# Opening of a gated-attention + GELU-FFN kernel on one Trainium2 core: hand-written engine orders, weight conversion as a stream, visits in two halves

## Chip, cores, metric

The kernel runs on one core of one Trainium2 chip. The metric is device time in microseconds (us). The kernel before took 604.11 us in the median of three runs (602.83 to 604.21). Engines are named as the profile names them: PE (TensorE), DVE (VectorE), ACT (ScalarE), POOL (GpSimd), SP (SyncE, which issues most of the transfers).

## What is computed

A linear attention with a decay per channel runs over 768 time steps for 4 batches and 8 heads of 48 channels; its output, seen as 3072 tokens of 384 channels, goes through a feed-forward network with an exact GELU. All in fp32.

```python
# attention, per batch and head, D = 48
state = alpha[t][:, None] * state + outer(k[t], v[t])
y[t]  = q[t] @ state
# FFN on x = y as 3072 x 384
h = x @ w_in                                   # 384 x 2048
g = 0.5 * h * (1 + erf(h / sqrt(2)))
out = g @ w_out                                # 2048 x 384
```

The weights reach the chip as float64 and are turned to fp32 pairs there.

## The kernel before, in words

**Groups, pairs, visits.** Time is cut into 12 groups of 256 steps (three groups per batch), and the heads into 4 pairs. For every group `g` and pair `p` there are three pieces of attention work. `st0` (L200), which `ahead` (L398) calls, is the preparation: two scans of alpha on DVE (`pp` L203, `rp` L209), a tiny maximum and reciprocal between them (L205, L208), and two products that scale k and q in place (L210, L212; from group 3 on the product for q is on POOL). A `visit` (L376) then works on three pairs at once, as a pipeline of depth three: for the newest pair `scores` and `turned` (PE, into the PSUM tile `s`), then `out_of_scores` (DVE mask product `ss` L240, ACT copy `kn` L247); for the pair before it `inside` (PE, into `ybank`) and `chain` (four small DVE adds `state` L318 to L322); for the pair before that `outside_part` (PE into `ybank`), `carry` (DVE L327) and `out_of_y` (ACT cast L365 and DVE residual L366, which leave x as a high and a low part). After the last pair of a group the tile `z` is scattered into the three x tiles of the group by six transfers on SP (`x<-z` L372), and only then can the FFN of that group begin.

**FFN steps.** The FFN is a list of 96 steps. A step (`ffn_step` L571) takes one group and one eighth of d_ff: `gemm1` is 18 matmuls into `hp` (L413), ACT takes two GELUs of it (`ghi` L422, and in place L423), DVE makes the low part `glo` (L424), and `gemm2` is 12 matmuls into two accumulators `acc` (L435). `gemm2` of a step is issued after `gemm1` of the next one. When a span of steps of one group ends, DVE moves the accumulators into `part` (L451, or L447 where it adds). The first three groups share out their eighths in spans of 4, 2 and 2, so that the weights are needed late. From step 12 (slot 25) on, visits are slotted between the gemms at the positions of `FIRST_VISITS` and then at every fourth slot, two slots to a step.

**Weight conversion.** A piece is 768 KB of float64 (one eighth of w_in or of w_out); there are 16. `split_weights` (L170) loads a piece into the staging tile `st`, ACT rescales its upper words (`u` L179), six DVE instructions assemble the fp32 value and its low part (L180, L181, L184, L185, L186, and L188 for the low part), and ACT casts the high part between the last two (L187). The results are the tiles `wih`, `wil`, `woh`, `wol`.

**What sets the order.** The program is written in one order; a planner with a timeline model then sets the order of instructions on each engine, up to step 12 on all of them. From there (`ON_PE`, L575) PE keeps the order as written. Each engine runs its own queue in order, so an instruction that waits holds all that stands behind it on that engine. SP carries the transfers and small marker instructions that keep blocks of matmuls on `ybank` apart (L264).

Of the kernel before, what the change touches and what calls it, by code (L numbers as in the profile page):

```python
# [24 lines left out]
RC = 1  # L25
STAGE = 2
WARM = 22
XB = 4
ON_PE = 12
AHEAD = 3  # L30
FIRST_VISITS = (25, 28, 31, 34, 37, 40)
EVERY = 4


@with_exitstack
def gla_then_gelu_ffn(ctx: ExitStack, tc: tile.TileContext, q, k, v, alpha, w_in, w_out, out):
# [52 lines left out]
    n_checks = NG - GPB + GPB * NPAIR // RC  # L89
# [52 lines left out]
    stage = stage_cm.__enter__()  # L142

# [26 lines left out]
    def split_weights(src, hi, lo, name):  # L170
        st = stage.tile([P, 2 * DM], I64, tag="st", name=f"st_{name}")
        nc.sync.dma_start(st.rearrange("p (two e) -> p two e", two=2), src)
        hi, lo = (x.rearrange("p two e -> p (two e)") for x in (hi, lo))
        top = st.bitcast(I32)[:, 1::2]
        mid = st.bitcast(U16)[:, 1::4]
        u = stage.tile([P, 2 * DM], F32, tag="u", bufs=1, name=f"u_{name}")
        w = stage.tile([P, 2 * DM], F32, tag="w", bufs=2, name=f"w_{name}")
        ui, wi = u.bitcast(I32), w.bitcast(I32)
        nc.scalar.activation(u, st.bitcast(F32)[:, 1::2], AF.Copy, scale=2.0**-112)  # L179
        nc.vector.tensor_scalar(out=ui, in0=ui, scalar1=3, scalar2=None, op0=ALU.logical_shift_left)  # L180
        nc.vector.scalar_tensor_tensor(  # L181
            out=wi, in0=top, scalar=SIGN, in1=ui, op0=ALU.bitwise_and, op1=ALU.bitwise_or
        )
        nc.vector.tensor_scalar(out=ui, in0=wi, scalar1=SIGN_EXP, scalar2=None, op0=ALU.bitwise_and)  # L184
        nc.vector.scalar_tensor_tensor(out=u, in0=mid, scalar=2.0**-36, in1=u, op0=ALU.mult, op1=ALU.mult)  # L185
        nc.vector.tensor_tensor(out=w, in0=w, in1=u, op=ALU.add)  # L186
        nc.scalar.copy(hi, w)  # L187
        nc.vector.tensor_tensor(out=lo, in0=w, in1=hi.bitcast(F32), op=ALU.subtract)  # L188
# [187 lines left out]
    def visit(now):  # L376
# [12 lines left out]
        if inner:  # L389
            chain(*inner)  # L390
# [286 lines left out]
```

## Time and profile before

| what | value |
|---|---|
| median of three runs | 604.11 us (602.83 to 604.21) |
| the profiled execution, own time / span of its instructions | 604.35 us / 602.8 us |
| busy: PE, DVE, ACT, POOL | 520.0, 326.9, 207.3, 45.3 us |
| first 161.2 us: PE, DVE busy; granted clock of TensorE | 84.5, 138.4 us; 0.69 |
| 170.2 to 597.0 us: PE, DVE busy; granted clock | 426.5, 185.5 us; 1.00 |

The page gives the span in 40 slices with the busy share of each engine in tenths and the granted TensorE clock; the groups of instructions by line; and the waits. In the timeline views an instruction has a start, a duration and, in brackets, the idle time in front of it with what ended it. Consecutive DVE instructions overlap by some hundredths of a microsecond in these records, so the distance between two starts is a little less than the duration.

### The profile page before, as it was taken

The numbers are of one execution on the slowest core, as the hardware profiler recorded it, in microseconds if no ns is written. First come the engines' busy times: TensorE is split into PE (matmuls) and PEld (weight loads), VectorE is DVE, ScalarE is ACT, GpSimd is POOL, SyncE is SP. The second block draws the span as 40 slices with busy tenths as digits, with TensorE's granted clock in tenths as the row PEclk, the third lists the DMA queues.
The fourth block names the chain that finished last, engine by engine and source line by source line (L and its number), as shares of the span: only waits on it lengthen the run. The fifth ranks groups of instructions, "written<-read, shape, count | busy, mean of one in ns | idle before, by whom it ended". The sixth has DMA issues, their size and how long they took to land.

```text
span 602.8 us, 14257 instructions
## 1 busy us (share of the span) xinstructions
PE 520.0 (86%) x5966; PEld 497.9 (83%) x5966; DVE 326.9 (54%) x793; ACT 207.3 (34%) x411; POOL 45.3 (8%) x69
## 2 busy tenths in 40 slices
PE   5343683396499999999999999999999999999996
PEld 5222672286499999999999999999999999999995
DVE  8898899897513565743555447436554532222111
ACT  6534542442222234343242343432422422222221
POOL 4000001011000012100101001001010000000000
PEclk9555795589599999999999999999999999999999
DMA  8633534351200103211122022111210200000000
GB/s 197 170 122 98 163 105 145 104 185 41 78 1 2 41 25 110 69 47 48 53 81 67 21 61 67 44 49 56 81 47 29 73 28 11 5 27 14 28 1 30
DMA packets 27542, 39.53 MB, mean 66 GB/s; under 512 B 4016, under 2 KB 21344, under 8 KB 27472
## 3 DMA queue, kind: packets, MB, share of 16 engines
q1 hardware_dynamic: 26240, 34.23, 20.0%
q0 software_dynamic: 1232, 4.33, 2.0%
q8 instruction: 49, 0.80, 0.6%
q14 instruction: 21, 0.17, 0.1%
HBM read 31.46 MB, written 4.72 MB: 60 GB/s over the span
## 4 chain that ended last, share of the span: by engine, by line
PE 77%; DVE 12%; DMA 5%; ACT 2%; issue 2%; SPq 1%; POOL 1%; DVEq 0%; ACTq 0%; POOLq 0%
PE hp L413 33%; PE acc L435 32%; PE ybank L341 3%; DMA ad<-in_alpha_dram 3%; PE s L233 2%; PE ybank L284 2%; PE s L226 2%; PE ybank L298 2%; DMA qd<-in_q_dram 2%; DVE pp L203 1%; DVE rp L209 1%; DVE u_i L185 1%; DVE wol L188 1%; DVE w_i L181 1%; DVE u_o L185 1%
## 5 line engine op out<-in xcount | busy, mean ns | idle before, releaser
L413 PE MATMUL hp<-x,wih 128*128 128x256 f32 x1152 | 213.0, 286 | 13.5 <-DMA x<-z 13.5
L413 PEld LDWEIGHTS hp<-x,wih 128*128 128x128 f32 x1152 | 185.2, 192 | 14.3 <-DMA x<-z 8.9
L424 DVE TENSOR_TENSOR glo<-hp,ghi 128x512 fp32r<-128x512 f32 x96 | 66.1, 689 | 186.8 <-ACT hp L423 186.6
L413 PE MATMUL hp<-x,wil 128*128 128x256 f32 x576 | 163.7, 284 | 0.0
L422 ACT ACTIVATE ghi<-hp 128x512 fp32r<-128x512 f32 x96 | 57.3, 596 | 237.3 <-PE hp L413 237.3
L435 PE MATMUL acc<-woh,ghi 128*128 128x384 f32 x384 | 133.0, 347 | 2.1 <-ACT ghi L422 2.1
L435 PE MATMUL acc<-woh,glo 128*128 128x384 f32 x384 | 129.5, 339 | 0.2 <-DVE glo L424 0.2
L435 PE MATMUL acc<-wol,ghi 128*128 128x384 f32 x384 | 129.6, 337 | 0.0
L413 PEld LDWEIGHTS hp<-x,wil 128*128 128x128 f32 x576 | 112.2, 195 | 0.1
L435 PEld LDWEIGHTS acc<-woh,ghi 128*128 128x128 f32 x384 | 72.3, 189 | 2.8 <-ACT ghi L422 2.4
L435 PEld LDWEIGHTS acc<-woh,glo 128*128 128x128 f32 x384 | 72.6, 189 | 0.5 <-DVE glo L424 0.3
L435 PEld LDWEIGHTS acc<-wol,ghi 128*128 128x128 f32 x384 | 72.6, 189 | 0.0
L423 ACT ACTIVATE hp<-hp 128x512 f32<-128x512 f32 x96 | 56.9, 593 | 0.0
L341 PE MATMUL ybank<-qd,state 48*48 48x64 f32 x704 | 32.8, 235 | 27.6 <-DVE x L366 19.1
L212 POOL TENSOR_TENSOR qd<-qd,pp 128x256 f32<-128x256 f32 x36 | 30.1, 859 | 332.5 <-DMA qd<-in_q_dram 284.8
L341 PEld LDWEIGHTS ybank<-qd,state 48*48 48x48 f32 x704 | 25.0, 130 | 36.3 <-DVE x L366 21.6
L226 PE MATMUL s<-qd,kd 48*64 48x64 f32 x768 | 26.6, 244 | 28.1 <-ACT kn L247 18.1
L226 PEld LDWEIGHTS s<-qd,kd 48*64 48x64 f32 x768 | 19.4, 148 | 31.0 <-ACT kn L247 25.6
L203 DVE TENSOR_TENSOR_SCAN pp<-ad,top 128x256 f32<-128x256 f32 x48 | 30.7, 680 | 19.4 <-DMA ad<-in_alpha_dram 19.3
L209 DVE TENSOR_TENSOR_SCAN rp<-ad,rp,top 128x255 f32<-128x255 f32 x48 | 39.6, 864 | 0.0
L247 ACT COPY kn<-s 128x256 f32<-128x256 f32 x48 | 17.8, 371 | 59.7 <-DVE ss L240 59.7
L284 PE MATMUL ybank<-vn,kn 64*64 64x48 f32 x704 | 23.4, 242 | 3.7 <-DVE z L366 3.0
(70 smaller groups left out, 442.2 us busy)
## 6 DMA issues: line engine op xcount, KB each, us to landing
st_i<-in_moe_w_in_dram SPq DMA_DIRECT2D x8, 768.0 KB, 4.3
st_o<-in_moe_w_out_dram SPq DMA_DIRECT2D x8, 768.0 KB, 4.5
vn<-in_v_dram SPq DMA_DIRECT2D x12, 384.0 KB, 3.4
out_dram<-part POOLq DMA_DIRECT2D x11, 384.0 KB, 2.9
ad<-in_alpha_dram SPq DMA_DIRECT2D x40, 96.0 KB, 2.5
kd<-in_k_dram SPq DMA_DIRECT2D x40, 96.0 KB, 2.4
qd<-in_q_dram SPq DMA_DIRECT2D x40, 96.0 KB, 2.3
x<-z SPq DMA_DIRECT2D x72, 32.0 KB, 2.0
```

What stands on the lines that cost most here:

```text
L203: nc.vector.tensor_tensor_scan(pp, at, top, MID, ALU.mult, ALU.min)
L209: nc.vector.tensor_tensor_scan(rp[:, G - 2 :: -1], at[:, G - 1 : 0 : -1], top[:, 1:], end, ALU.mult, ALU.min)
L212: q_eng.tensor_tensor(out=qt, in0=qt, in1=pp, op=ALU.mult)
L226: nc.tensor.matmul(d["s"][o, h, c * CS : (c + 1) * CS], lhsT=d["kt"][r, t], rhs=d["qt"][r, t], start=True, stop=True)
L247: nc.scalar.copy(kn, d["s"][:, 0, C : C + 2 * C].rearrange("p (c d) -> p c d", c=2))
L284: in_block(nc.tensor.matmul(y[o, b, u0 + c * D : u0 + (c + 1) * D], lhsT=d["kn"][r, c, o], rhs=vbuf[g % NB][r, c, e : e + D], start=(c == ...
L341: in_block(nc.tensor.matmul(y[r, b, c * CS : (c + 1) * CS], lhsT=states[p][j][r], rhs=d["qt"][r, j * CS : (j + 1) * CS], start=False, stop ...
L413: nc.tensor.matmul(hp[:, j, :], lhsT=a[:, j, i * P : (i + 1) * P], rhs=x[:, i, :], start=(i == 0 and n == 0), stop=(i == NK - 1 and n == 2),)
L422: nc.scalar.activation(ghi, hp, AF.Gelu)
L423: nc.scalar.activation(hp, hp, AF.Gelu)
L424: nc.vector.tensor_tensor(out=glo, in0=hp, in1=ghi.bitcast(F32), op=ALU.subtract)
L435: nc.tensor.matmul(acc[t], lhsT=a[:, j, ts], rhs=w[:, j, :], start=(first and j == 0 and n == 0), stop=(last and j == 1 and n == 2),)
```

## The change

1. From the first instruction up to the end of step 14, PE, DVE, ACT and SP keep the order as written (`by_hand`); POOL and everything later are left to the planner, and PE keeps its written order from there on.
2. `split_weights` becomes `convert`, one generator over all 16 pieces. `fill(n)` issues the next n DVE instructions of it (96 in all; the ACT work and the load of the piece three further on go with them). The low part of a piece comes two instructions into the next piece. One product is written back into the staging tile instead of `u`; three staging tiles instead of two.
3. A visit issues its matmuls at once and returns `rest`, which issues its DVE and ACT half later, with `fill` and the next preparation between the two halves. `carry` moves into `rest`.
4. `low` (the DVE part of a step) is separated from `gemm1`, so that a step can have `fill` in front of it.
5. Group 0 has 12 conversion instructions between its visits, its four steps 38; group 1 has none; the visits of group 2 run inside the four steps of group 1 with 15; seven further steps (8 to 14) have 35 (of which the last few find the stream empty). Later visits move from slots 25, 28, ... 40 to 35, 37, ... 57.
6. The range check of alpha is made once per group instead of once per pair for the first groups. The ring of x tiles has three buffers instead of four, and every fourth group's x lives in a tile that takes the room of the staging pool once this is closed.

```diff
-RC = 1
-STAGE = 2
+STAGE = 3
-XB = 4
-ON_PE = 12
+XB = 3
-FIRST_VISITS = (25, 28, 31, 34, 37, 40)
+FIRST_VISITS = (35, 37, 39, 41, 43, 45, 47, 50, 53, 57)
+FILL = 5
...
-    def split_weights(src, hi, lo, name):
...
+    def convert():
+        behind = None
+        u = scaled(0)
+        for n, (_, hi, lo) in enumerate(pieces):
...
+            nc.vector.tensor_scalar(out=ui, in0=ui, scalar1=3, scalar2=None, op0=ALU.logical_shift_left)
+            yield
+            nc.vector.scalar_tensor_tensor(
+                out=wi, in0=top, scalar=SIGN, in1=ui, op0=ALU.bitwise_and, op1=ALU.bitwise_or
+            )
+            yield
+            if behind:
+                nc.vector.tensor_tensor(**behind, op=ALU.subtract)
+                yield
+            nc.vector.tensor_scalar(out=ui, in0=wi, scalar1=SIGN_EXP, scalar2=None, op0=ALU.bitwise_and)
+            yield
+            nc.vector.scalar_tensor_tensor(out=r, in0=mid, scalar=2.0**-36, in1=u, op0=ALU.mult, op1=ALU.mult)
+            if n + 1 < len(pieces):
+                u = scaled(n + 1)
+            yield
+            nc.vector.tensor_tensor(out=w, in0=w, in1=r, op=ALU.add)
+            fetch(n + STAGE)
+            nc.scalar.copy(flat(hi), w)
+            behind = dict(out=flat(lo), in0=w, in1=flat(hi).bitcast(F32))
+            yield
...
     def x_tiles(g):
-        x = ffn.tile([P, NK, 2, G], F32R, tag="x", bufs=XB, name=f"x{g}")
+        if g != "s" and g % (XB + 1) == XB:
+            x = late[0].tile([P, NK, 2, G], F32R, tag="xl", name=f"x{g}")
+        else:
+            x = ffn.tile([P, NK, 2, G], F32R, tag="x", bufs=XB, name=f"x{g}")
...
+        def rest():
+            if now:
+                out_of_scores(*now)
+            if inner:
+                chain(*inner)
+            if outer:
+                carry(*outer)
+                out_of_y(*outer)
...
+    by_hand.enter_context(tc.manual_schedule(engines={ET.PE, ET.DVE, ET.Activation, ET.SP}))
+    load_data(0, (0, 1), False)
+    fetch(0)
+    load_data(0, (1, NPAIR))
+    fetch(1)
     load_data(1)
+    fetch(2)
+    ahead(0, 0, False)
+    rest = visit((0, 0))
+    ahead(0, 1, False)
+    for p in range(2, NPAIR):
+        rest()
+        rest = visit((0, p - 1))
+        fill(2)
+        ahead(0, p, False)
...
     for f in range(4):
-        ffn_step()
...
+        ffn_step(lambda f=f: fill(12 if f < 3 else 2))
...
+    for p in range(NPAIR):
+
+        def during(p=p):
+            rest = visit((2, p))
+            if p == 0:
+                ahead(2, 3, False)
+            else:
+                fill(3)
+            rest()
+
+        ffn_step(during)
...
+    for _ in range(7):
+        ffn_step(lambda: fill(FILL))
+    by_hand.close()
+    stage_cm.__exit__(None, None, None)
+    late.append(ctx.enter_context(tc.tile_pool(name="late", bufs=1, side="right")))
```

**Place 1: DVE, from the end of group 0's attention to its first FFN step.** Before, the last residual of group 0 (`z`) stands among conversions, preparations and visit work of group 1 (`pp_2`, `pp_3`, `state`, `ss_2`):

```order
L366 TENSOR_TENSOR z_487<-ybank,z_487 128x256
L188 TENSOR_TENSOR wil_178<-w_i_592,wih_170 128x768
L180 TENSOR_SCALAR u_o_603<-u_o_603 128x768
L181 SCALAR_TENSOR_TENSOR w_o_604<-st_o_601,u_o_603 128x768
L203 SCALAR_TENSOR_TENSOR pp_2_1121<-ad_116,top 128x256
L203 SCALAR_TENSOR_TENSOR pp_3_1214<-ad_116,top 128x256
L320 TENSOR_TENSOR state_1_144<-ybank,state_0_143 128x48
L240 TENSOR_TENSOR ss_2_834<-s_2_806,mask 128x256
```

With the change the same residual comes after only two converted pieces and no work of group 1, and behind it stands nothing but the stream of conversions up to the first `glo`:

```order
L401 TENSOR_TENSOR z_486<-ybank,z_486 128x256
L203 SCALAR_TENSOR_TENSOR w_483<-st_232,u_463 128x768
L208 TENSOR_TENSOR wol_192<-w_416,woh_184 128x768
L210 TENSOR_SCALAR u_463<-w_483 128x768
L212 SCALAR_TENSOR_TENSOR st_232<-st_232,u_463 128x768
L216 TENSOR_TENSOR w_483<-w_483,st_232 128x768
L201 TENSOR_SCALAR u_531<-u_531 128x768
L203 SCALAR_TENSOR_TENSOR w_537<-st_413,u_531 128x768
L208 TENSOR_TENSOR wil_177<-w_483,wih_169 128x768
```

**Place 2: DVE, where group 1 goes into the FFN.** Before, the copies of the finished accumulators of group 0 (`part_203`) stand in the midst of visit work of group 1, well ahead of the end of its attention:

```order
L320 TENSOR_TENSOR state_3_151<-ybank,state_2_150 128x48
L451 COPY part_203<-acc_0_503 128x384
L451 COPY part_203<-acc_0_504 128x384
L184 TENSOR_SCALAR u_i_1299<-w_i_1300 128x768
L322 TENSOR_TENSOR state_4_152<-ybank,state_3_151 128x48
```

With the change they stand right behind the last residual of group 1 (`z_976`). On PE the `gemm2` that they wait for stands behind the first `gemm1` of group 1, which needs the transfers of `z_976`. Behind the copies stand the preparation of group 2's last pair (`pp_3_1042`) and preparations of group 3 (`pp_0_1767`, `pp_1_1814`):

```order
L359 TENSOR_SCALAR state_0_158<-state_4_162,pe_3_830 128x48
L401 TENSOR_TENSOR z_976<-ybank,z_976 128x256
L490 COPY part_203<-acc_0_502 128x384
L490 COPY part_203<-acc_0_503 128x384
L235 SCALAR_TENSOR_TENSOR pp_3_1042<-ad_116,top 128x256
L235 SCALAR_TENSOR_TENSOR pp_0_1767<-ad_120,top 128x256
L235 SCALAR_TENSOR_TENSOR pp_1_1814<-ad_120,top 128x256
```

**Place 3: DVE in the steps of group 2 (steps 8 to 11).** Before, only the low parts and the accumulator copies are left for DVE there:

```order
L424 TENSOR_TENSOR glo_0_1397<-hp_0_1377,ghi_0_1396 128x512
L424 TENSOR_TENSOR glo_1_1447<-hp_1_1427,ghi_1_1446 128x512
L424 TENSOR_TENSOR glo_2_1495<-hp_2_1475,ghi_2_1494 128x512
L424 TENSOR_TENSOR glo_3_1543<-hp_3_1523,ghi_3_1542 128x512
L451 COPY part_205<-acc_8_1375 128x384
```

With the change five conversion instructions stand between each two of them:

```order
L462 TENSOR_TENSOR glo_0_1403<-hp_0_1383,ghi_0_1402 128x512
L216 TENSOR_TENSOR w_1420<-w_1420,st_1122 128x768
L201 TENSOR_SCALAR u_1426<-u_1426 128x768
L203 SCALAR_TENSOR_TENSOR w_1468<-st_1293,u_1426 128x768
L208 TENSOR_TENSOR wol_197<-w_1420,woh_189 128x768
L210 TENSOR_SCALAR u_1426<-w_1468 128x768
L462 TENSOR_TENSOR glo_1_1449<-hp_1_1429,ghi_1_1448 128x512
```

The seven steps 8 to 14 hold 31 conversion instructions in this way, which before stood ahead of step 8.

More of the change, by code (lines that the diff above doesn't have):

```diff
@@ L168, in range_check @@
             )
-    def split_weights(src, hi, lo, name):
[L171 to L188, printed above, removed]
@@ new lines, in fetch, with flat, scaled @@
+    def fetch(n):
+        if n >= len(pieces):
+            return
+        staged[n] = stage.tile([P, 2 * DM], I64, tag="st", name=f"st_{n}")
+        nc.sync.dma_start(staged[n].rearrange("p (two e) -> p two e", two=2), pieces[n][0])
+    def flat(x):
+        return x.rearrange("p two e -> p (two e)")
+    def scaled(n):
+        u = stage.tile([P, 2 * DM], F32, tag="u", bufs=1, name=f"u_{n}")
+        nc.scalar.activation(u, staged[n].bitcast(F32)[:, 1::2], AF.Copy, scale=2.0**-112)
+        return u
@@ L198, in gla_then_gelu_ffn, with fill @@
+    stream_w = convert()
+    def fill(n):
+        for _ in range(n):
+            next(stream_w, None)
     cur = {}
@@ L534, in general_path @@
             for f in range(NF2):
-                gh, gl = gemm1("s", f)
+                gh, gl, low = gemm1("s", f)
+                low()
                 gemm2("s", f, gh, gl, acc, f == 0, f == NF2 - 1, f == NF2 - 1, n0)
@@ L578, in ffn_step @@
             stream["acc"] = [ps_o.tile([P, DM], F32, tag=f"acc{t}", name=f"acc{t}_{i}") for t in range(2)]
-        gh, gl = gemm1(g, f)
+        gh, gl, low = gemm1(g, f)
+        if now is None:
+            low()
         for fn in slots[2 * i]:
@@ L586, in ffn_step @@
             fn()
-    load_data(0, (0, 1, NPAIR))
-    ahead(0, 0)
-    load_w_in(0)
-    visit((0, 0))
-    ahead(0, 1)
-    visit((0, 1))
-    load_data(1)
-    ahead(0, 2)
-    load_w_out(0)
-    visit((0, 2))
-    ahead(0, 3)
-    visit((0, 3))
-    visit(None)
-    visit(None)
-    for f in range(4):
-        ffn_step()
-        if f < 3:
-            quad(f + 1)
-    for g in range(1, NSB):
-        for pair in pairs_of(g):
-            ahead(*pair)
-            visit(pair)
-            if g > 1:
-                ffn_step()
-        visit(None)
-        visit(None)
+        if now is not None:
+            now()
+            low()
@@ new lines, in gla_then_gelu_ffn @@
+    for turn in range(2):
+        fill(3)
+        rest()
+        rest = visit(None)
+    fill(2)
+    rest()
+    for f in range(4):
+        ffn_step(lambda f=f: fill(12 if f < 3 else 2))
+        if f == 0:
+            range_check(data[0]["a"])
+    ahead(1, 0, False)
+    rest = visit((1, 0))
+    for p in range(1, NPAIR):
+        ahead(1, p, False)
+        rest()
+        rest = visit((1, p))
+    range_check(data[1]["a"])
+    for p in range(2):
+        ahead(2, p, False)
+        rest()
+        rest = visit(None)
@@ new lines, in gla_then_gelu_ffn @@
+    ahead(2, 2, False)
+    rest()
+    for p in range(NPAIR):
[4 more added lines that the diff above has]
+            else:
+                fill(3)
+            rest()
+        ffn_step(during)
+    range_check(data[0]["a"])
+    for turn in range(2):
+        rest = visit(None)
+        fill(3)
+        rest()
+    for _ in range(7):
+        ffn_step(lambda: fill(FILL))
+    by_hand.close()
+    stage_cm.__exit__(None, None, None)
```

68 lines of the change are left out of this document (32 added, 36 removed).

## Prediction

> **What bounds the kernel now.** I read the slices of the page first, then the busy time by stretch, then the chain and the waits.
>
> ```profile
> PE   5343683396499999999999999999999999999996
> DVE  8898899897513565743555447436554532222111
> PEclk9555795589599999999999999999999999999999
> ```
>
> PE is full from the eleventh slice on (about 161 us) and mostly empty and at half clock ahead of it; there DVE is the full engine.
>
> ```profile
> 0.00:15.00 15.00, 8.32 (x62) 7.82 (x62) 12.26 (x33) 9.90 (x22) 6.87 (x22) 0.94 0.80 197
> 75.00:90.00 15.00, 13.61 (x124) 11.91 (x123) 13.71 (x23) 6.03 (x10) 0.00 (x0) 1.00 0.34 105
> 90.00:105.00 15.00, 4.38 (x98) 3.32 (x102) 14.19 (x32) 3.90 (x6) 2.12 (x2) 0.55 0.44 145
> 120.00:135.00 15.00, 13.64 (x128) 12.13 (x127) 13.65 (x25) 6.13 (x11) 2.48 (x2) 0.81 0.58 195
> 0.00:161.20 161.20, 84.47 (x1045) 72.03 (x1045) 138.42 (x301) 67.82 (x133) 14.13 (x28) 0.69 0.43 126
> 170.20:597.00 426.80, 426.49 (x4874) 416.95 (x4873) 185.53 (x487) 136.77 (x273) 29.73 (x39) 1.00 0.15 42
> ```
>
> The columns are length, PE, PE weight loads, DVE, ACT, POOL, clock, DMA share, GB/s. In the first 161.2 us DVE works 138.4 (86%); from 170.2 to 597.0 PE works all of it, DVE 43%. So the end is set by when PE becomes dense and by how many FFN steps are behind it then.
>
> ```profile
> 161.18 6.93 PE hp L413 x36
> 168.11 2.09 PE acc L435 x12
> 170.20 2.12 PE hp L413 x18
> 592.62 4.18 PE acc L435 x24
> ```
>
> A full-clock step is 2.12 + 2.09 = 4.21 us. At 170.2 ten gemm1 are done (ahead of 162 us stand eight `glo`, in the row of L424 below, so eight steps; the row x36 is the 18 matmuls of step 8 and the 18 of step 9) and nine gemm2. My mark is "15 gemm1 and 14 gemm2 done, twelve pairs done, all visits of group 3 to come", where the change's hand order ends. Before, it stands at 170.2 + 5 × 4.21 = 191.2 (I leave out visit work there), and from it to the span's end are 602.8 − 191.2 = 411.6 us. That remainder is the same work after the change, on a full PE. The prediction is thus one number: when the new order reaches the mark.
>
> **Prices on DVE.** In a written order an instruction that needs the one in front of it pays its whole recorded duration.
>
> ```profile
> L209 DVE TENSOR_TENSOR_SCAN rp<-ad,rp,top 128x255 f32<-128x255 f32 x20 | 14.2, 749 | 0.0
> L203 DVE TENSOR_TENSOR_SCAN pp<-ad,top 128x256 f32<-128x256 f32 x20 | 12.9, 682 | 9.1 <-DMA ad<-in_alpha_dram 9.1
> L210 DVE TENSOR_TENSOR kd<-kd,rp 128x256 f32<-128x256 f32 x18 | 7.0, 414 | 0.0
> L181 DVE SCALAR_TENSOR_TENSOR w_i<-st_i,u_i 128x768 int32<-128x768 int32 x8 | 7.6, 947 | 0.0
> L185 DVE SCALAR_TENSOR_TENSOR u_i<-st_i,u_i 128x768 f32<-128x768 uint16 x8 | 8.1, 1007 | 0.1
> L184 DVE TENSOR_SCALAR u_i<-w_i 128x768 int32<-128x768 int32 x8 | 4.4, 551 | 0.0
> L208 DVE RECIPROCAL rp<-pe 128x1 f32<-128x1 f32 x20 | 2.5, 152 | 0.0
> L320 DVE TENSOR_TENSOR state<-ybank,state 128x48 f32<-128x48 f32 x32 | 6.3, 198 | 0.5 <-PE ybank L298 0.3
> L424 DVE TENSOR_TENSOR glo<-hp,ghi 128x512 fp32r<-128x512 f32 x8 | 5.5, 687 | 2.3 <-ACT hp L423 2.1
> ```
>
> A preparation: 0.68 + 0.75 + two products of 0.41 + two tiny ones of about 0.15 = 2.5 us. A converted piece: two instructions like L184 and four like L181 or L185, 1.1 + 3.9 = 5.0 at full durations; I take 4.9, since the low part of the piece before stands between two of them. The DVE half of a visit ("tail"): mask product and residual like L210, four state adds and the carry as a fifth, 1.8, with a little for the hop from ACT 1.9. A low part: 0.6 from start to start. A hand-over from `z` to the FFN:
>
> ```profile
> 58.70 0.41 DVE L366 TENSOR_TENSOR z<-ybank,z 128x256 fp32r<-128x256 f32 x1
> 112.95 0.42 DVE L366 TENSOR_TENSOR z<-ybank,z 128x256 fp32r<-128x256 f32 x1
> 156.74 0.42 DVE L366 TENSOR_TENSOR z<-ybank,z 128x256 fp32r<-128x256 f32 x1 [1.62 <-ACT z L365]
> 156.40 0.79 SPq L150 DMA_DIRECT2D ad<-in_alpha_dram  x2
> 157.28 3.68 SPq L372 DMA_DIRECT2D x<-z  x6
> 161.18 0.77 PE L413 MATMUL hp<-x,wih 128*128 128x256 f32 x2 [4.91 <-DMA x<-z]
> 161.96 0.63 PE L413 MATMUL hp<-x,wih 128*128 128x256 f32 x2
> 162.60 0.63 PE L413 MATMUL hp<-x,wih 128*128 128x256 f32 x2
> 159.02 1.27 DVE L203 TENSOR_TENSOR_SCAN pp<-ad,top 128x256 f32<-128x256 f32 x2 [1.85 <-DMA ad<-in_alpha_dram]
> 71.48 0.60 ACT L422 ACTIVATE ghi<-hp 128x512 fp32r<-128x512 f32 x1
> 87.63 1.01 DVE L451 COPY part<-acc 128x384 f32<-128x384 f32 x2
> 143.97 0.55 DVE L451 COPY part<-acc 128x384 f32<-128x384 f32 x1
> ```
>
> From the end of `z` (157.2) to the first matmul 4.0 us; then three matmuls take 0.64, so a cold gemm1 of 18 takes 3.9; the two GELUs after it take 0.6 each.
>
> **The sum, stage by stage.** *Group 0's attention (to 35.1).* The first scan starts at 5.1 as before. Four preparations 10.0, two pieces 9.8 (place 1: nothing of group 1 any more), four tails 7.6. Pairs 1 to 3 are now queued behind a 768 KB piece instead of the 384 KB of v: at the 197 GB/s of the first row 2 us later. In all I put 2.6 on DVE's wait for loads; below, 1 if ACT and PE let it run on; above, 5. Before, `z` of group 0 came at 58.7.
> *Its four steps (to 69.0).* 38 conversion instructions 31.0, four low parts 2.4, 0.5 for waits. First matmul at 39.1; the cold gemm1 and two GELUs end when `fill` reaches the low part, so that wait hides.
> *Group 1's attention (to 94.1).* Seven preparations 17.5, four tails 7.6; PE's half of a visit hides under the next preparation.
> *Place 2 (to 105.1).* A new wait: the accumulator copies wait on DVE for a gemm2 that stands on PE behind the first gemm1 of group 1. 4.0 + 3.9 + about 2.6 for the gemm2 (2.09 warm, twice that cold) + 0.5 for the second copy = 11.0. Queued behind it are the preparation of group 2's last pair, its mask product and the next low part, thus PE's next gemm2. Before, the copies (87.6) waited for nothing. Nothing hides this; its bounds are 9 and 13.
> *Steps 4 to 7 with group 2's visits (to 142.6).* One preparation 2.5 and six of groups 3 and 4 without the product for q at 1.85 (2.1, less what two of them save by standing interleaved; 11.1; the planner still hoists them in here), 15 conversion instructions 12.3, four tails 7.6, four low parts 2.4: 35.9, and 1.6 for residuals that wait for an ACT cast. Bounds 34 and 42, the upper by POOL (below).
> *The second hand-over (to 153.6).* 11.0 again for the copies of group 1. The two last preparations of group 4 stand ahead of them; their alpha is issued behind the six `x<-z` (3.7 us) and lands 2.6 later, as 159.02 follows 156.40 before, so they end near 152.7 and hide in that wait; without it they would cost 3.7.
> *Steps 8 to 13 (to 186.4).* Place 3: 30 conversion instructions 24.5, six low parts 3.6, two copies 1.0, 2.0 for their wait on PE: 31.1, to 184.7, and the rest of a gemm2, 1.7. PE alone would need 6 × 4.21 = 25.3; here DVE paces it at 5 us a step. Bounds 28 and 37.
>
> The mark stands at 186.4 instead of 191.2: 4.8 us sooner. Span 186.4 + 411.6 = 598.0; the profiled execution has 604.35 − 602.8 = 1.55 beside its span, so **599.5 us**; against the median of 604.11 (0.24 under that execution) it is 0.8% less.
>
> **Parts at nothing.** Fewer range checks take ACT time, of which 93 of the first 161 us are idle. The strided write of L185's successor into the staging tile: nothing, since L181 reads that tile with a stride at the pace of the others; if it cost a quarter more, 16 × 0.25 = 4 us. The fourth x in the staging room needs the last conversion (step 14) and is first written by group 3's visits, 4 steps or 17 us later; uncovered, it would hold group 3's cast. Group 3's `z` now comes two gemms and a visit (about 7 us) ahead of its first gemm1, against a path of 4.0 plus cast and residual and up to 2.2 for load issues in front of it on SP: nothing, at most 1.5.
>
> **A clock rule.** Two rows of gemm2 in the half-empty stretch:
>
> ```profile
> 129.49 0.52 PE L435 MATMUL acc<-wol,ghi 128*128 128x384 f32 x1
> 129.81 0.84 PE L435 MATMUL acc<-woh,glo 128*128 128x384 f32 x2
> 136.31 0.34 PE L435 MATMUL acc<-woh,glo 128*128 128x384 f32 x1
> ```
>
> At 129.5 starts are 0.32 us apart; at 136.3 the record is 0.34 long and PE is at full clock. With PE 91% busy in both windows, the mean clock was 0.81 in 120 to 135 and 1.00 in 75 to 90. The Trainium skill ("TensorE: Matmul & The Clock Gate", Part 1) says that about 3.4 us of idleness lead to the half clock and as much activity back; by that rule pauses of 1 us in steps 8 to 13 leave the clock full and the sum stands. The same page (HAM oscillation, second failure mode) tells of frequent micro-idling that makes the clock swing; that would be the third rival.
>
> **Rivals.** *Written order costs less than I say, 590 us.* If DVE loses nothing to dependent neighbours, each saves about 0.08 (one copy at 143.97 takes 0.55, the two at 87.63 together 1.01): a piece costs 4.45 and a preparation 2.1, 16 × 0.45 + 11 × 0.4 = 11.6 less, of which the hand-overs give back 2. For it: DVE's records in the half-empty stretch overlap like that. Against: the new order puts dependent ones next to each other.
> *The hand-overs and POOL eat it, 603.5.* POOL's products slow DVE:
>
> ```profile
> 121.61 2.48 POOL L212 TENSOR_TENSOR qd<-qd,pp 128x256 f32<-128x256 f32 x2 [21.81 <-DMA qd<-in_q_dram]
> 122.13 1.37 DVE L185 SCALAR_TENSOR_TENSOR u_i<-st_i,u_i 128x768 f32<-128x768 uint16 x1
> 123.53 1.38 DVE L186 TENSOR_TENSOR w_i<-w_i,u_i 128x768 f32<-128x768 f32 x1
> ```
>
> Beside two of them two instructions took 0.4 longer each. Eight fall into the hand-ordered stretch, two of them in a wait: 6 × 0.45 = 2.7, and 1.3 for the longer gemm2 in two cold hand-overs: 4.0 of the 4.8 are gone.
> *Slower: the paced steps lose the clock, 612.* In steps 8 to 13 PE pauses in every step. At half clock a step takes 3.9 + 12 × 0.32 = 7.7 instead of 5.0, and PE paces: six steps 16 more, 615.7; with most of them, 612. It decides from two such steps on (5.4 > 4.8). For it the 0.52 rows; against it window 75 to 90.
> *The order doesn't hold:* the planner still puts preparations of later groups into it; that is counted.
>
> **How the numbers follow.** Forecast (faster by 0.3 to 1.6%) 0.35; cheap order 0.23; eaten 0.18; paced at half clock 0.24, in which I count any other chain of waits as dear. About 0.3% (1.8 us) is what a measurement of this kernel can tell. Faster 0.35 + 0.23 = 0.58; same 0.18; slower 0.24. The bounds of the stages add to −12 and +17 where all fall together; taking in the rivals to one tenth on each side, the range is 586 to 612; the forecast's own is 594 to 603.
>
> **What would show it.** DVE's `z` of groups 0, 1, 2 at 35, 94, 143 (before 58.7, 113.0, 156.7); the first `hp` at 39, 98 and 147; DVE idle for some 10 us in front of the copies to `part`, twice; steps 8 to 13 5 us apart with the clock at 1.00; from some 188 us PE full. Wrong would be: `z` of group 2 later than 152, gemm2 records of 0.5 us after 155, or PE pausing after 190.

## The result and the profile after

The changed kernel takes 630.66 us (median of four runs, 629.56 to 631.65) against 603.62 us for the kernel before on the same chip (four runs, 602.83 to 604.21). The ratio is 1.045 with a 95% interval of 1.043 to 1.047: 27 us slower. Forecast was 599.5 us, with 586 to 612 as range. Both the sign and the range were wrong. The profiled execution of the changed kernel has a span of 629.0 us. One execution of a later run (all edits together) took 865.33 us at a granted clock of 0.55, where its nine others took 603 to 609, and is left out of that run's median.

The slices of its page:

```profile
PE   6445743781588999799999999999999999999996
DVE  5868986676587347455434554555346542331211
PEclk9557865895688999899999999999999999999998
```

A slice is 15.7 us. PE is full only from the fourteenth slice (about 204 us), and three slices later it shows a 7, with an 8 in the clock below it, where the kernel before shows nothing but 9s up to its last slice.

Rows of DVE that end the stages of the prediction, with the waits in front of them (start, duration, engine, line):

```profile
11.31 0.69 DVE L235 TENSOR_TENSOR_SCAN pp<-ad,top 128x256 f32<-128x256 f32 x1 [3.59 <-DMA ad<-in_alpha_dram]
...
38.30 0.42 DVE L401 TENSOR_TENSOR z<-ybank,z 128x256 fp32r<-128x256 f32 x1 [0.54 <-ACT z L400]
...
49.39 0.56 DVE L201 TENSOR_SCALAR u<-u 128x768 int32<-128x768 int32 x1 [6.47 <-ACT u L189]
...
77.60 0.68 DVE L462 TENSOR_TENSOR glo<-hp,ghi 128x512 fp32r<-128x512 f32 x1
...
105.13 0.42 DVE L401 TENSOR_TENSOR z<-ybank,z 128x256 fp32r<-128x256 f32 x1
114.63 0.56 DVE L490 COPY part<-acc 128x384 f32<-128x384 f32 x1 [9.08 <-PE acc L474]
115.67 0.56 DVE L490 COPY part<-acc 128x384 f32<-128x384 f32 x1 [0.48 <-PE acc L474]
...
157.93 0.42 DVE L401 TENSOR_TENSOR z<-ybank,z 128x256 fp32r<-128x256 f32 x1 [1.17 <-ACT z L400]
164.99 1.27 DVE L235 TENSOR_TENSOR_SCAN pp<-ad,top 128x256 f32<-128x256 f32 x2 [6.64 <-DMA ad<-in_alpha_dram]
...
169.46 1.01 DVE L490 COPY part<-acc 128x384 f32<-128x384 f32 x2
...
201.31 0.68 DVE L462 TENSOR_TENSOR glo<-hp,ghi 128x512 fp32r<-128x512 f32 x1
```

And two rows of PE: the start of the gemm2 of step 13, after the gemm1 of step 14, and the first matmul after that gemm2. The second one is the mark of the prediction (15 gemm1 and 14 gemm2 done).

```profile
202.74 0.33 PE L474 MATMUL acc<-woh,ghi 128*128 128x384 f32 x1
...
204.83 0.40 PE L449 MATMUL hp<-x,wih 128*128 128x256 f32 x2
```

The prediction was one number in two parts: when the mark is reached, and 411.6 us behind it. By its own stages:

| stage | predicted, us | measured, us | difference |
|---|---|---|---|
| group 0's attention, from the first scan at 5.1 | 30.0 | 33.6 | +3.6 |
| its four steps, to the last low part | 33.9 | 39.6 | +5.7 |
| group 1's attention | 25.1 | 27.3 | +2.2 |
| first hand-over, to the end of the copies | 11.0 | 10.7 | −0.3 |
| steps 4 to 7 with group 2's visits | 37.5 | 42.1 | +4.6 |
| second hand-over | 11.0 | 12.1 | +1.1 |
| steps 8 to 13, to the last low part | 31.1 | 31.5 | +0.4 |
| to the mark | 1.7 | 2.8 | +1.1 |
| behind the mark | 411.6 | 424.2 | +12.6 |
| span | 598.0 | 629.0 | +31.0 |

So 18.4 us of the miss lie in the opening and 12.6 us behind it, in the part that I had carried over unchanged. All three signs that the prediction had named as wrong came: `z` of group 2 later than 152 (157.9), gemm2 records of 0.5 us after 155 (0.53 at 198.86), and PE pausing after 190 (2.66 us at 194.6). What PE waited for after 200 us (kernel after; total, times, longest):

```profile
PE acc L474 <- DVE glo L462: 5.3, 6, 1.5
PE ybank L316 <- SPq L296: 3.2, 1, 3.2
PE ybank L373 <- DVE x L401: 0.9, 1, 0.9
```

The kernel before has no such wait behind 200 us. These three come to 9.4 of the 12.6 us. Behind the wait of 3.2 the clock is 0.71 in the window from 256.2 to 262.0, that is some 3.4 us at half clock, worth 1.7 (last section). And my 411.6, extrapolated from one step, was about 1.4 short: two versions below need 415.2 and 414.2 us behind the mark with waits of PE of 2.2 and 1.2, thus 413.0 of full work both. With these three parts the 12.6 are accounted for.

### The profile page after: what moved, and what is told of

It reads as the page before. It is cut to its first block, busy times and chain, and to the rows that moved or that the text cites. A ratio compares the mean times of both kernels' runs of the same rounds, so it can differ in the third digit from the quotient of the medians.

```text
span 629.0 us, 14203 instructions
## 1 busy us (share of the span) xinstructions
PE 529.2 (84%) x5966; PEld 502.2 (80%) x5966; DVE 336.6 (54%) x793; ACT 201.2 (32%) x375; POOL 45.0 (7%) x69
## 4 chain that ended last, share of the span: by engine, by line
PE 66%; DVE 19%; DMA 5%; issue 3%; SPq 3%; ACT 2%; POOL 1%; DVEq 0%; ACTq 0%; POOLq 0%
PE acc L474 28%; PE hp L449 26%; DMA ad<-in_alpha_dram 5%; PE ybank L373 3%; PE s L265 2%; DVE rp L241 2%; DVE pp L235 2%; PE ybank L316 2%; PE s L258 2%; PE ybank L330 2%; DVE st L212 2%; SPq L407 2%; DVE glo L462 2%; DVE w L203 1%; DVE w L216 1%
## 5 line engine op out<-in xcount | busy, mean ns | idle before, releaser
L449 PE MATMUL hp<-x,wih 128*128 128x256 f32 x1152 | 222.8, 294 | 27.5 <-DMA x<-z 18.9
L449 PEld LDWEIGHTS hp<-x,wih 128*128 128x128 f32 x1152 | 188.7, 199 | 29.2 <-DMA x<-z 13.4
L449 PE MATMUL hp<-x,wil 128*128 128x256 f32 x576 | 167.1, 290 | 3.1 <-DVE wil L208 3.1
L474 PE MATMUL acc<-woh,glo 128*128 128x384 f32 x384 | 132.4, 345 | 16.6 <-DVE glo L462 16.5
L474 PE MATMUL acc<-woh,ghi 128*128 128x384 f32 x384 | 130.7, 340 | 0.0
L449 PEld LDWEIGHTS hp<-x,wil 128*128 128x128 f32 x576 | 115.1, 200 | 3.8 <-DVE wil L208 3.8
L373 PEld LDWEIGHTS ybank<-qd,state 48*48 48x48 f32 x704 | 25.3, 133 | 42.1 <-DVE x L401 26.9
L373 PE MATMUL ybank<-qd,state 48*48 48x64 f32 x704 | 33.0, 238 | 29.5 <-DVE x L401 24.2
L235 DVE TENSOR_TENSOR_SCAN pp<-ad,top 128x256 f32<-128x256 f32 x48 | 31.1, 679 | 34.5 <-DMA ad<-in_alpha_dram 34.5
L352 DVE TENSOR_TENSOR state<-ybank,state 128x48 f32<-128x48 f32 x128 | 26.0, 203 | 27.8 <-PE ybank L330 25.8
L241 DVE TENSOR_TENSOR_SCAN rp<-ad,rp,top 128x255 f32<-128x255 f32 x48 | 37.9, 817 | 0.4
L490 DVE COPY part<-acc 128x384 f32<-128x384 f32 x23 | 12.6, 553 | 39.6 <-PE acc L474 39.6
```

The costliest lines, as they stand in the source:

```text
L235: nc.vector.tensor_tensor_scan(pp, at, top, MID, ALU.mult, ALU.min)
L241: nc.vector.tensor_tensor_scan(rp[:, G - 2 :: -1], at[:, G - 1 : 0 : -1], top[:, 1:], end, ALU.mult, ALU.min)
L352: nc.vector.tensor_tensor(out=st[j + 1], in0=u, in1=st[j], op=ALU.add)
L373: in_block(nc.tensor.matmul(y[r, b, c * CS : (c + 1) * CS], lhsT=states[p][j][r], rhs=d["qt"][r, j * CS : (j + 1) * CS], start=False, stop ...
L449: nc.tensor.matmul(hp[:, j, :], lhsT=a[:, j, i * P : (i + 1) * P], rhs=x[:, i, :], start=(i == 0 and n == 0), stop=(i == NK - 1 and n == 2),)
L474: nc.tensor.matmul(acc[t], lhsT=a[:, j, ts], rhs=w[:, j, :], start=(first and j == 0 and n == 0), stop=(last and j == 1 and n == 2),)
```

## The experiments

All times are medians, with the ratio to the kernel before measured on the same chip. The changed kernel is at 630.7 us throughout. A gain is the difference of two medians; the runs stand on several chips, on which the kernel before took 603.6 to 605.1 us, so that by the ratios the gains come out differently by up to 1.4 us (in the run on loads by 2.5).

### The later visits on even half-steps

```diff
-FIRST_VISITS = (35, 37, 39, 41, 43, 45, 47, 50, 53, 57)
+FIRST_VISITS = (35, 37, 39, 41, 43, 45, 47, 50, 53, 56)
```

A step has two slots, or half-steps, for visits: an even number is between its gemm1 and the gemm2 issued after it, an odd number behind that gemm2. Preparations stand three numbers earlier, so they take the other place. With EVERY = 4 the last number decides for all later groups: 40 before the change, 57 after.

> Only the last number of FIRST_VISITS is 56 instead of 57, so that all later visits fall between a step's gemm1 and its gemm2 as they did before the change, and the preparations, three half-steps ahead, fall behind a gemm2. Theory A (place in the step): the six waits of PE for glo behind 290 us (5.3 us in total in the changed kernel) go, 630.7 becomes about 625.4. Theory B (the visit's own new order, with the carry last, makes glo late): the waits stay, 630.7 within 1.

Measured: 624.67 us, ratio 1.034 (1.028 to 1.040): 6.0 us shorter. Of PE's waits for low parts behind 200 us none above 0.3 us is left; the marker's and the residual's stay. Behind the mark the profiled execution needs 419.4 us instead of 424.2. Theory A holds. The rows of DVE in the changed kernel show what an odd number does. Two preparations that were waiting for one load run as a block right before the low part that PE's next gemm2 needs:

```profile
310.76 1.27 DVE L235 TENSOR_TENSOR_SCAN pp<-ad,top 128x256 f32<-128x256 f32 x2 [2.42 <-DMA ad<-in_alpha_dram]
...
314.07 0.66 DVE L462 TENSOR_TENSOR glo<-hp,ghi 128x512 fp32r<-128x512 f32 x1
```

```profile
314.79 0.45 PE L474 MATMUL acc<-woh,glo 128*128 128x384 f32 x1 [1.51 <-DVE glo L462]
```

DVE stood 2.42 us for the load and then worked 3.3 us on preparations. The GELUs of the low part behind them were done at 309.9, and PE wanted it at 313.28 (314.79 less 1.51): without the block in front of it there would have been no wait, which the run on the even place bears out. The preparations are not urgent: the visit that uses them comes three half-steps later.

### The same place in the kernel before

```diff
-FIRST_VISITS = (25, 28, 31, 34, 37, 40)
+FIRST_VISITS = (25, 28, 31, 34, 37, 41)
```

> The kernel before, with the last number of FIRST_VISITS 41 instead of 40, so that its visits from group 4 on fall behind a gemm2 and the preparations between a gemm1 and its gemm2. Theory A (the place in the step alone costs the late part 5 us): 604 becomes 608 to 611, with waits of PE for glo of 4 to 7 us in the trace. Theory B (it takes the changed visit to make glo late): 603 to 605.

Measured: 613.55 us, ratio 1.016 (1.011 to 1.021): one number in a table costs 9.6 us. In the waits of PE behind 200 us there is now one row, where the kernel before has none:

```profile
PE acc L435 <- DVE glo L424: 6.6, 7, 1.7
```

About 2.8 us more are in the opening, where the first matmul of step 8 comes at 164.02 instead of 161.18; why is open. The time lies above the 608 to 611 of Theory A, but the waits are those that it names (4 to 7 us): it holds for the late part, without any of the changed code.

### The visits of group 3 earlier and less crowded

```diff
-FIRST_VISITS = (35, 37, 39, 41, 43, 45, 47, 50, 53, 57)
+FIRST_VISITS = (33, 35, 37, 39, 41, 43, 46, 49, 52, 56)
```

In the changed kernel the six x<-z of group 3 stand on SP between two visits that are two half-steps apart. Each visit's matmuls wait for a marker on SP's queue, and the `x<-z` and two loads stand in front of it. Rows of SP and of PE:

```profile
250.31 4.68 SPq L407 DMA_DIRECT2D x<-z  x6
255.09 0.53 SPq L150 DMA_DIRECT2D qd<-in_q_dram  x1
255.66 0.42 SPq L156 DMA_DIRECT2D vn<-in_v_dram  x1
```

```profile
256.20 0.45 PE L316 MATMUL ybank<-vn,kn 64*64 64x48 f32 x16 [3.18 <-SPq L296]
```

> FIRST_VISITS (33, 35, 37, 39, 41, 43, 46, 49, 52, 56): group 3's visits two half-steps earlier, three half-steps instead of two between the visit that issues its x<-z and the next one, and all later visits on even half-steps. Theory A (two causes, the odd place and the crowded six x<-z in front of the marker): against the kernel with only the last number changed (624.7) the wait of 2.9 us on SP's marker and about 1.2 of half clock behind it go too, 620 to 621. Theory B (the marker's wait only moves to another visit, or group 3's earlier visits hit the conversion's end): 624 to 626.

Measured: 619.91 us, ratio 1.025 (1.022 to 1.028), 4.8 us less than with the even place alone and 10.8 us less than the changed kernel. PE's waits behind 200 us:

```profile
PE ybank L316 <- SPq L296: 1.1, 1, 1.1
PE ybank L373 <- DVE x L401: 0.9, 1, 0.9
PE acc L474 <- DVE pe L237: 0.2, 1, 0.2
```

The marker's wait shrinks from 3.2 to 1.1 us, and only 0.2 us turn up elsewhere. Behind the mark (204.69) the profiled execution needs 415.2 us, 9.0 less than the changed kernel. Theory A holds: most of the 12.6 us behind the opening come from two places in the table.

### Conversions ahead of step 0

```diff
-    for f in range(4):
-        ffn_step(lambda f=f: fill(12 if f < 3 else 2))
+    fill(5)
+    for f in range(4):
+        ffn_step(lambda f=f: fill(7 if f == 0 else 12 if f < 3 else 2))
```

The rows of ACT in the changed kernel show why:

```profile
47.47 0.60 ACT L458 ACTIVATE ghi<-hp 128x512 fp32r<-128x512 f32 x1 [7.90 <-PE hp L449]
...
48.48 0.88 ACT L189 ACTIVATE u<-st 128x768 f32<-128x768 f32 x1
```

The first operation of the next piece, `u`, has its data and its tile from 41.9 us on. It is written behind the GELUs of step 0, and these wait for a gemm1 that waits for the hand-over of x. So ACT stands for 7.9 us, and DVE, which needs `u`, for 6.5.

> Five of the twelve conversion instructions of step 0 are written ahead of its gemm1, so that ACT's u of the next piece and the cast of the piece before stand in front of the two GELUs of step 0 and no longer behind them. DVE's order is the same. Theory A (ACT's order is the cause): DVE's wait of 6.47 us for u goes and the whole is about 6 us shorter, 624.7. Theory B (DVE only waits elsewhere, since PE's cold gemm1 of step 0 sets the next low part): 0 to 2 us shorter, 629 to 630.7.

Measured: 624.89 us, ratio 1.033 (1.027 to 1.039): 5.8 us shorter. The longest of DVE's waits for `u` falls from 6.5 to 1.6 us. Theory A holds.

### The last gemm2 ahead of the next group, with and without moved conversions

```diff
+    def flush(take):
+        gemm2(*stream["pend"], take=take)
+        stream["pend"] = None
 ...
+    take = []
     for p in range(1, NPAIR):
+        if p == 1:
+            flush(take)
         ahead(1, p, False)
+        if p == 2:
+            take.pop()()
 ...
+    fill(8)
     for p in range(NPAIR):
 ...
+    flush(take)
     for turn in range(2):
         rest = visit(None)
         fill(3)
+        if turn == 0:
+            take.pop()()
         rest()
+    fill(8)
     for _ in range(7):
```

With `take` given, gemm2 writes its matmuls at once and its two accumulator copies where `take.pop()()` stands. This is the first version, with FILL = 3; the second leaves both `fill(8)` out and keeps FILL = 5.

> The last gemm2 of groups 0 and 1 in the opening is written ahead of the next group's visits instead of behind the next group's first gemm1, its accumulator copies a preparation or a fill later, and eight conversion instructions stand in each hand-over (FILL 3 instead of 5 in the seven steps behind). Theory A (the copies' wait on PE is lost DVE time): the waits of 9.1 and 6.6 us shrink to 3 or less each and the whole is 10 to 14 us shorter, 617 to 621. Theory B (the hand-over z to x to gemm1 sets the pace whatever DVE does in it): at most 4 us, 627 or more.

> As in the hand-over run the last gemm2 of groups 0 and 1 stands ahead of the next group's visits and its copies a preparation or a fill later, but no conversion is moved into the hand-overs (FILL stays 5). Theory A (half of the gain is DVE work put into the hand-over, the other half the copies that no longer stand in front of preparations): 3 to 6 us shorter than the changed kernel, 625 to 628; the hand-over run had 618.8. Theory B (the copies' place is all of it): 618 to 620. Theory C (only the moved conversions count): 630 to 631.

Measured: 618.78 us, ratio 1.026 (1.018 to 1.034), with the moved conversions; 615.43 us, ratio 1.018 (1.014 to 1.021), without. The first number is the one that Theory A of the first run had, but the second shows that its reason does not hold: the place of the gemm2 and of its copies is worth 15.2 us alone. That is the reason of Theory B of the second run, and more than its 618 to 620 allowed. Putting conversions into the hand-overs loses some 3 us of it (the intervals of the two ratios overlap a little, so the size is rough). The rows of `z` of group 2 and of the first gemm1 behind it tell why, first with the moved conversions, then without:

```profile
152.47 0.42 DVE L401 TENSOR_TENSOR z<-ybank,z 128x256 fp32r<-128x256 f32 x1
```

```profile
157.19 0.80 PE L449 MATMUL hp<-x,wih 128*128 128x256 f32 x2 [5.82 <-DMA x<-z]
```

```profile
147.42 0.42 DVE L401 TENSOR_TENSOR z<-ybank,z 128x256 fp32r<-128x256 f32 x1 [1.17 <-ACT z L400]
```

```profile
151.82 0.80 PE L449 MATMUL hp<-x,wih 128*128 128x256 f32 x2 [6.88 <-DMA x<-z]
```

Eight conversions (6.6 us) ahead of step 4 push group 2's chain 5 us back. They were not missed behind: without them the preparations of group 2's last pair and of group 3 fill the first hand-over. In the seven steps at the end PE needs 29.5 us (7 × 4.21) whatever DVE does, so taking work off DVE there gives little. My reading of the 9.1 us as DVE time that conversions should fill was wrong; the wait was dear because preparations and the next low part stood behind it.

### Loads and range check

```diff
-    fetch(0)
     load_data(0, (1, NPAIR))
+    fetch(0)
 ...
                 ahead(2, 3, False)
+                range_check(data[0]["a"])
 ...
-    range_check(data[0]["a"])
     for turn in range(2):
```

In the changed kernel the range check behind step 7 reads an array into which group 4's first two pairs are then loaded, so that ACT stands for that load with the casts of group 2 behind it.

> The load of group 0's pairs 1 to 3 is issued ahead of the first 768 KB weight piece, and the range check of group 2 stands behind its last preparation in step 4 instead of behind step 7. Theory A: DVE's wait of 3.6 us at 7.7 shrinks to 1.5 and the two waits of 1.1 for ACT's casts behind the checks go, about 4 us in all, 626 to 627. Theory B (the first piece is late by as much, and the casts only wait for the later load): within 1 us of 630.7.

Measured: 630.41 us, ratio 1.040 (1.035 to 1.046): no gain that four executions between 625.44 and 633.64 can show. DVE's wait of 3.59 us for pair 1's alpha is gone and that for the first weight piece has grown from 1.37 us by almost as much:

```profile
10.38 0.43 DVE L244 TENSOR_TENSOR qd<-qd,pp 128x256 f32<-128x256 f32 x1 [0.36 <-DMA qd<-in_q_dram]
...
15.61 0.56 DVE L201 TENSOR_SCALAR u<-u 128x768 int32<-128x768 int32 x1 [4.47 <-ACT u L189]
```

That is Theory B. My reading, which no run isolates, is that the queue order only decides who waits, and the bytes in front of group 0 set the sum. The residual of pair 2 no longer waits a microsecond for ACT's cast (0.16 instead of 1.08), but that of `z` does as before (1.17): what stands ahead of its cast on ACT is the work on a weight piece, not the range check.

### The planner instead of the written order

```diff
-    by_hand.enter_context(tc.manual_schedule(engines={ET.PE, ET.DVE, ET.Activation, ET.SP}))
```

> The same code without the hand order for the opening: the planner sorts the same instructions, loads, staging room and conversion stream. Theory A (the written order itself costs, since it can't fill a wait): the opening is as long as before the change (mark at 191 instead of 205) and the time 613 to 620. Theory B (what was changed beside the order, the staging of the data, the staged conversion and the larger loads, costs): 626 or more.

Measured: 631.10 us, ratio 1.043 (1.037 to 1.048). Theory A falls: the planner needs as much for this code as the written order. The number is that of Theory B, but its reason (staging, conversion stream, larger loads) is not what the runs below show, since the fastest version keeps all of these at 602 us. The shapes of the two differ. Windows from 120 to 160 us, first the kernel before, then the planned run (columns as in the prediction), and the planned run's `z` of group 2:

```profile
120.00:160.00 40.00, 26.24 (x282) 23.27 (x280) 31.14 (x60) 12.53 (x21) 5.14 (x4) 0.80 0.30 96
```

```profile
120.00:160.00 40.00, 27.68 (x292) 24.73 (x288) 18.12 (x44) 8.75 (x17) 1.43 (x2) 0.73 0.12 31
```

```profile
169.88 0.42 DVE L401 TENSOR_TENSOR z<-ybank,z 128x256 fp32r<-128x256 f32 x1 [1.62 <-ACT z L400]
```

The planned run has DVE busy for 18.1 of these 40 us, where the kernel before has 31.1, and its `z` comes 13 us later. In the text of the changed kernel most conversions stand ahead of the attention of groups 1 and 2, and the planner seems to have followed that; this is read from the two windows, and no run shows it.

### All edits together, and the ones that gained

The first of these holds every edit above: the conversions ahead of step 0, the hand-over with its moved conversions, the loads and the check, and the earlier visits.

> All of these together: five conversions ahead of step 0, last gemm2 and eight conversions in each hand-over, the earlier load and check, and the visits as in the run with both late edits. Theory A (the waits are separate and add up): 630.7 less 6 (ACT's order), 12 (hand-over), 3 (load and check) and 10 (late visits) is 600, at most 603: as the kernel before or a little faster. Theory B (one wait's removal uncovers the next): 606 to 612.

Measured: 605.51 us, ratio 1.001 (0.998 to 1.004): as the kernel before, and between the theories, nearer to B. By themselves the edits had given 5.8, 11.9, 0.3 and 10.8, so 601.9 was to be had if they added up; 3.6 us of 28.8 are uncovered again. The next one leaves out the two edits that had not gained (the moved conversions, and the loads with the check).

> The three edits that each gained, together: five conversions ahead of step 0, the last gemm2 of groups 0 and 1 ahead of the next group's visits without moved conversions (FILL 5), and the visits as in the run with both late edits. Theory A (separate waits, their gains add): 630.7 less 5.8, 15.3 and 10.8 is 598.8, 596 to 601, faster than the kernel before by about 1%. Theory B (one removal uncovers the next, as when all edits stood together): 603 to 608.

Measured: 602.26 us, ratio 0.997 (0.994 to 0.999). This is the fastest version, 0.3% under the kernel before. The three gains would have given 598.9 by their sum; 3.4 of 31.8 us are uncovered again. The time lies between the two theories: the gains add, but not in full. Its first gemm1 of step 8 is 12.3 us earlier than the 161.18 of before:

```profile
148.85 0.79 PE L449 MATMUL hp<-x,wih 128*128 128x256 f32 x2 [6.89 <-DMA x<-z]
...
177.72 0.45 PE L474 MATMUL acc<-woh,glo 128*128 128x384 f32 x1 [2.65 <-DVE glo L462]
```

and its mark is reached at 185.3, only 6 us earlier than the 191.2 of before. The seven steps behind the hand-over, which would take 4.21 us each on a full PE, are paced by DVE's conversions (PE waits 3.6 us for low parts there) and cost half the head start. Two more runs tried to win that back.

```diff
-FILL = 5
+FILL = 4
 ...
-    for _ in range(7):
+    for _ in range(9):
         ffn_step(lambda: fill(FILL))
```

> As the run before it, with the rest of the conversion dealt out four to a step over nine steps instead of five over seven, since DVE and not PE paces the seven steps (4.9 us a step beside PE's 4.21). Theory A (DVE paces there): 2 to 4 us less than that run, 594 to 598. Theory B (the nine steps are paced by the copies and casts in DVE's order, or group 3's first visits now collide with the conversion): the same or up to 2 us more.

Measured: 606.99 us, ratio 1.004 (1.002 to 1.007): 4.7 us worse, more than either theory had. The low part of step 14 does come 2.6 us sooner (184.25 instead of 186.83), but something else has moved. Preparations of groups 3 and 4, which the planner had put into DVE's gaps up to the second hand-over, now come behind the longer written order, and DVE has gaps where they were and a crowd later. Rows of DVE:

```profile
154.69 0.69 DVE L462 TENSOR_TENSOR glo<-hp,ghi 128x512 fp32r<-128x512 f32 x1 [7.38 <-ACT hp L459]
...
191.74 2.34 DVE L235 TENSOR_TENSOR_SCAN pp<-ad,top 128x256 f32<-128x256 f32 x3
```

and windows of the same run, in which PE was full in the run before (15.00 of 15 in both):

```profile
180.00:195.00 15.00, 11.00 (x89) 10.05 (x88) 13.41 (x25) 2.94 (x6) 3.18 (x4) 1.00 0.00 1
195.00:210.00 15.00, 11.23 (x101) 10.18 (x101) 13.85 (x38) 2.58 (x6) 4.02 (x5) 0.77 0.00 1
```

DVE did pace the seven steps, as Theory A has it; but the collision with group 3 that Theory B names costs more than that.

```diff
                 ahead(2, 3, False)
             else:
-                fill(3)
+                fill(4)
 ...
-FILL = 5
+FILL = 4
```

> As the run with the three gainful edits, and each of steps 5 to 7 takes four conversions instead of three, so that the seven steps behind need four each instead of five (3 + 28 are the 31 left). Theory A (in steps 5 to 7 DVE waits 1.4 to 2.0 us a step for PE's scores, so that a conversion of 0.8 there is free, and the seven steps, paced by DVE at 4.9 us, come to PE's 4.3): 3 to 4 us less than 602.3, 598 to 600. Theory B (the scores' wait only moves behind the conversion, as when eight conversions were put into each hand-over): 601 to 604.

Measured: 603.52 us, ratio 0.999 (0.997 to 1.001). DVE's waits for PE's scores did shrink (longest 1.1 us instead of 2.0), but the next alpha loads are waited for longer: 4.29 and 4.27 us, where the version with the three edits has 0.68 and 2.90.

```profile
136.03 1.27 DVE L235 TENSOR_TENSOR_SCAN pp<-ad,top 128x256 f32<-128x256 f32 x2 [4.29 <-DMA ad<-in_alpha_dram]
...
152.57 1.27 DVE L235 TENSOR_TENSOR_SCAN pp<-ad,top 128x256 f32<-128x256 f32 x2 [4.27 <-DMA ad<-in_alpha_dram]
```

Even so the mark comes 1.9 us sooner, at 183.37 instead of 185.29: the steps are faster, as Theory A has it. The loss is behind the mark. With five instructions to a step the stream left one for step 14; with four to a step it leaves four, the last of which waits for ACT's cast, and PE waits 3.2 us for the low part behind them, where the version with the three edits has no wait above 0.6 behind its mark:

```profile
187.60 0.96 DVE L221 TENSOR_TENSOR wol<-w,woh 128x768 fp32r<-128x768 f32 x1 [1.01 <-ACT woh L218]
```

```profile
189.21 0.67 PE L474 MATMUL acc<-woh,glo 128*128 128x384 f32 x1 [3.21 <-DVE glo L462]
```

The time is in the range of Theory B: one removal uncovers the next wait, though not the one that it names.

## Why the prediction was wrong

**The remainder was not the same.** The step that failed first is "that remainder is the same work after the change, on a full PE". The work is the same, its places are not. I had read the new FIRST_VISITS as a question of when group 3 is ready, and did not ask on which side of the gemm2 the later visits fall. It cost 6.0 us by the run on the even place, and the same edit in the kernel before costs 6.6 us of PE's waits there (9.6 in all). The prediction said that group 3's close visits cost "nothing, at most 1.5": the run with earlier visits gains 4.8 us there. I had counted the load issues in front of x<-z, not the six x<-z in front of the next visit's marker.

**The step "so that wait hides" was wrong.** For step 0 I compared the end of gemm1 with the time at which DVE reaches the low part, and forgot that ACT's queue is written too. DVE never reached the low part: it stood 6.5 us at the next piece's first instruction, because ACT was held at the GELUs. The run with conversions ahead of step 0 puts 5.8 us on this one place.

**The hand-overs had the right size and the wrong remedy.** For the first I said 11.0, measured were 10.7, with the wait at the copies as described. In the second the preparations of group 4 stand ahead of the copies, as I wrote, but it is their wait that is not hidden: DVE stands 6.6 us at their load, and the copies behind find their sums ready; 12.1 instead of 11.0. I had called the cost what nothing hides, which was right; written elsewhere, the two give 15.2 of their 22.8 back.

**Waits in steps 4 to 7** were undersized: the stage took 42.1 for 37.5, at its upper bound of 42. I had 1.6 us for ACT's casts and nothing else. The trace has 3.1 for casts (0.44, 0.44, 1.08, 1.17), 3.0 for a load that comes just too late, and 2.7 for PE's scores (1.30 and 1.40); DVE's own work was 2.6 cheaper than I said. That group 1's attention took 27.3 for 25.1 is of the same kind: some 2 us of waits for scores and casts, which I had called hidden.

**The first stage** was 3.6 over. Its waits for loads are 3.6 for alpha plus 1.4 for `u`, together the 5 of my upper bound, where I had put 2.6; the rest is waits of 0.3 to 0.5 us for scores and casts that I had left out.

**Terms without a bound.** I gave bounds to the stages that I doubted, and none to the four steps of group 0, to group 1's attention and to the remainder. These three hold 20.5 of the 31.0 us (5.7, 2.2 and 12.6), and the range of 586 to 612 left no room for them.

**What held.** The prices on DVE: a preparation takes 2.57 us (2.5), a converted piece 4.90 from the row at 59.64 to the one at 64.54 (4.9). So the rival "written order costs less" is out. The steps 8 to 13 took 31.5 us for 31.1. POOL's products slow a neighbour as seen before (a conversion of 1.35 us instead of 0.96) and decide nothing.

**The rivals.** Slower had 0.24, under the name of the half clock in the paced steps. The half clock came, but in single spells (below) and not in every step: the mean clock over steps 8 to 13 is 0.89, and their pace is the predicted one. What made it slower was in none of my mechanisms by name except "any other chain of waits", and that was too little for a written order on four queues. The error of method is that I followed DVE through the new order and took the other three queues as being on time.

The three edits that gained account for 5.8 + 15.2 + 10.8 = 31.8 us one by one and give 28.4 us together, where the loss was 27.0. So the cause of the loss is settled by runs: one place on ACT, two on PE and DVE, and the table of visits. That the time comes back where the waits are taken out, while the staging, the stream and the two halves of a visit stay, leaves these no large part in the loss. Open is why the planner takes 13 us longer to group 2's `z` with the changed code than before.

## What to carry to other kernels

When an order is written out for several engines, follow each queue by itself: an instruction that waits holds everything written behind it, also what is ready, and the price is paid by the engine that waits for that. A table of places is part of the order: a change of one number by one moved non-urgent work in front of an urgent instruction. A part called unchanged is only so when its places were compared, too.

## What the runs showed of the hardware

A pause of PE can be paid twice. In the changed kernel PE waits 2.66 us for a low part, from 194.6 to 197.25. Windows of 1 us behind it (columns as before; the clock is the third number from the end):

```profile
197.00:198.00 1.00, 0.75 (x4) 0.75 (x5) 1.00 (x3) 0.90 (x2) 0.00 (x0) 1.00 0.00 0
198.00:199.00 1.00, 1.00 (x7) 1.00 (x6) 1.00 (x3) 0.00 (x0) 0.00 (x0) 0.80 0.00 0
199.00:200.00 1.00, 1.00 (x6) 1.00 (x5) 0.96 (x2) 0.00 (x0) 0.00 (x0) 0.50 0.07 16
201.00:202.00 1.00, 1.00 (x6) 1.00 (x6) 0.99 (x2) 0.58 (x1) 0.00 (x0) 0.50 0.00 0
202.00:203.00 1.00, 1.00 (x10) 1.00 (x9) 0.00 (x0) 0.26 (x1) 0.00 (x0) 0.99 0.00 0
```

During the pause the clock is full (1.00 in the windows from 194 to 197). It is halved more than a microsecond after PE has gone on, and stays so for about 3.4 us of full work; the gemm1 in it, from 199.50 to 202.74, takes 3.2 us instead of 2.1. The pauses of 2.65 us in the fastest version (before the row at 177.72) and of 3.18 us behind the marker (before 256.20) are followed by the same.

The length of the pause alone does not decide it. In the run with conversions ahead of step 0 PE waits 2.67 us at the same place, and the clock stays full behind the pause:

```profile
190.23 0.45 PE L474 MATMUL acc<-woh,glo 128*128 128x384 f32 x1 [2.67 <-DVE glo L462]
```

```profile
192.00:193.00 1.00, 1.00 (x10) 1.00 (x9) 0.97 (x2) 0.00 (x0) 0.00 (x0) 1.00 0.00 0
```

In the run that moves the last gemm2 alone, a pause of 1.78 us, with PE full for 8 us up to 296, is followed by half clock:

```profile
298.30 0.45 PE L474 MATMUL acc<-woh,glo 128*128 128x384 f32 x1 [1.78 <-DVE glo L462]
```

```profile
299.00:300.00 1.00, 1.00 (x5) 1.00 (x5) 0.51 (x1) 0.00 (x0) 0.00 (x0) 0.50 0.00 0
```

So here a pause between 1.8 and 2.7 us may or may not be followed by half clock; what decides is not shown. Where it comes, 3.4 us at half clock do the work of 1.7, so that it costs up to 1.7 us more than the pause itself (an estimate from these rows). The Trainium skill ("TensorE: Matmul & The Clock Gate", Part 1) gives an idle window of about 3.4 us and as much activity back. The 3.4 us back agree with these rows; on the way down a shorter pause was enough, and the measurement decides.
